# The next expert's weights split into a second pair of tiles, and copied in where the expert begins

## The chip, the cores and the metric

The kernel runs on one core of a Trainium2 chip. The metric is the device time of one launch in microseconds (us). TensorE is called PE (its weight loads PEld), VectorE DVE, ScalarE ACT, GpSimd POOL; SP issues most DMAs.

## The reference

An attention with a decaying state runs over 4 sequences of 768 tokens (8 heads of 48), and its output, 3072 rows of 384, is the input of a mixture of experts: each token goes to the one expert of 8 with the highest logit.

```
for t in range(S):
    cur = einsum('bhd,bhe->bhde', u * k_t, v_t)
    y[:, :, t] = einsum('bhd,bhde->bhe', r_t, state + cur)
    state = w * state + einsum('bhd,bhe->bhde', k_t, v_t)
...
e_idx = argmax(x @ w_gate + modality_bias[modality_id], axis=1)
for e in range(E):
    mask = e_idx == e
    h = maximum(x[mask] @ w1[e], 0)
    out[mask] = gate_w[mask] * (h @ w2[e])
```

With the inputs of the reference only three experts get tokens (1569, 1354 and 149).

## The kernel before

The first 220 us compute the attention, the choice of the expert and a sort: rows are written to DRAM by expert. Weights and activations are used as pairs of fp16 tiles (a high part and the rest), so that products of fp32 inputs are made with fp16 matmuls. An expert's weights are 128 x 6144 fp32 in `raw` (the first 3072 columns are the first layer's, the others the second's). `split` makes `whi` on ACT (raw times a power of two, rounded) and `wlo` on DVE (the rest), in six pieces of 1024 columns (NQ = 6); `norm` (L917) is the sum of squares of a piece on ACT, from which `scales` gets the power of two.

A job is 128 tokens of one expert. Ten jobs of the expert guessed to be the largest are worked in during the attention (L1036 to L1072). The remaining ones are numbered 0 to 15 here: job 0 stands ahead of a loop, jobs 1 to 15 are its iterations, with a bound read at run time (L1451). At run time the experts are sorted by size, and each has at least two jobs. Here the first has jobs 0 to 2, the second 3 to 13, the third 14 and 15; jobs 3 and 14 are the switches.

`jobs` (L792 to L896) is a chain of small DVE operations that makes a table with a column for each job: the row in DRAM, a code, and the expert to load. In the code, 8 says that the next job begins an expert, 4 that this one does; 2 and 1 ask for the norms of the second and the first half of the next weights. One fp32 matmul (`ptab`, L891) spreads the table; it stands in PE's order between the high and the low terms of the last of the ten early jobs. `jobs` is a generator; L1371 to L1397 say which of its steps stand between which of the other work.

One iteration, in the order in which each engine gets it (the order is written by hand, L1451, and each engine follows its own):

- `turn` (L989): SP fetches and transposes the rows of the job after;
- `low_terms` (L1082) of the job before: 8 matmuls with `hl` and the second layer's `whi`, the last of its `po`;
- `second_half`: if an expert begins, the second layer's weights are split, on ACT, DVE and POOL; else norms, if asked for;
- `put` (L959): ACT takes `po` to `otb` (L966), POOL scatters it to the output;
- `next_load`: if an expert begins, SP loads the next one's weights;
- `due` (L1087): the factors of the rows, on DVE;
- `up` (L1017): three groups of first-layer matmuls (L1006, 4, 2 and 2 blocks), each followed by `hh` on ACT (L1010) and `hl` on DVE (L1015); `scales` (a small matmul `pw`, L931, and four DVE operations) in between;
- `take_in` (L1408): two DVE copies of the next job's rows;
- `high_terms` (L1074): 16 matmuls with `hh`, `whi` and `wlo` of the second layer;
- `first_half`: if the next job begins an expert, the first layer's weights are split (ACT and DVE).

The code is read into a register of ACT, DVE and POOL at L900 (`at`). An If is a comparison and a branch on each of these engines. Where an If is not taken, its engine executes a stand-in (ALU_OP and EVENT_SEMAPHORE rows at the line of the If's end) that does the semaphore updates of what was skipped, since others wait for counts. At the loop's end all engines meet (L1505) before the last `low_terms`.

## Time and profile before

| | us |
|---|---|
| three runs: lowest, median, highest | 364.02, 365.57, 366.82 |
| the profiled execution, its span | 368.68, 367.0 |
| PE busy in the span | 337.0 (92%), clock 0.976 |
| DVE, ACT, POOL busy | 228.1, 157.0, 173.1 |
| job 0, first matmul | 224.58 |
| loop, first to last job's `ids` (L1091, 16 times) | 224.2 to 355.0 |
| last `low_terms` | 360.19 |
| norms in the loop (L917) | 323.79 to 335.55 |

An instruction's row of the profile has its start in us from the span's start, its duration in us, its engine, its line, the operation and its tiles; x24 says that 24 were merged, and what stands in brackets is the idle time of the engine before it and what ended it. Rows with a q behind the engine are of its sequencer (branches, register operations, semaphores): count, shortest/median/longest duration in ns, first and last start.

### The profile page before, as it was taken

To read this page: it belongs to the slowest core of one execution; us is meant where nothing else is said; L and a number is where in the kernel's file an instruction comes from. 1 tells how busy PE (TensorE), PEld (TensorE's weight loads), DVE (VectorE), ACT (ScalarE), POOL (GpSimd) and SP (SyncE) were. 2 spreads that over 40 slices of the span, in tenths; PEclk is the share of its full clock that TensorE was granted. 3 is DMA by queue.
4 is the path that set the end of the run, shared out by engine and by line. 5 is a ranking of instruction groups with operands and counts; after the bars stand their busy time and mean duration, and the time that the engine had idled before them with its cause. 6 is when DMAs were issued, how large, how long until landed. Compare 5 with 4: busy or idle time off the path is not lost. (4 is left out here: it accounts for less than half of the span.)

```text
span 367.0 us, 14637 instructions
## 1 busy us (share of the span) xinstructions
PE 337.0 (92%) x5314; PEld 266.4 (73%) x5314; DVE 228.1 (62%) x754; ACT 157.0 (43%) x371; POOL 173.1 (47%) x252
## 2 busy tenths in 40 slices
PE   7969999799999989989989699997999999999883
PEld 3758888589797787958767577775777888777661
DVE  6997777588969767697657443349533333324960
ACT  7237657435257664636632022236222222256711
POOL 7985656847876697565333411125111121111811
PEclk9998999969999999999999789999999999999999
DMA  6948999769799997965851413114912212112120
GB/s 157 246 123 241 278 258 235 198 146 203 222 228 167 234 307 153 206 182 138 241 129 46 129 45 46 43 43 134 273 49 54 53 43 64 43 22 64 22 55 4
DMA packets 56091, 50.66 MB, mean 138 GB/s; under 512 B 40936, under 2 KB 49641, under 8 KB 55792
## 3 DMA queue, kind: packets, MB, share of 16 engines
q1 hardware_dynamic: 52848, 40.60, 49.3%
q0 software_dynamic: 3200, 9.47, 7.0%
q8 instruction: 30, 0.49, 0.6%
q14 instruction: 13, 0.11, 0.1%
HBM read 30.55 MB, written 11.63 MB: 115 GB/s over the span
## 5 line engine op out<-in xcount | busy, mean ns | idle before, releaser
L1006 PEld LDWEIGHTS <-whi 128*128 128x128 f16 x1248 | 73.3, 98 | 8.4 <-issue 5.5
L1080 PEld LDWEIGHTS <-hh 128*128 128x128 f16 x416 | 38.6, 99 | 31.7 <-ACT hh L1010 5.9
L1006 PE MATMUL phb<-mxT,whi 128*128 128x128 f16 x720 | 47.6, 219 | 0.0
L1006 PEld LDWEIGHTS <-wlo 128*128 128x128 f16 x624 | 38.3, 99 | 4.4 <-DVE wlo L952 3.1
L1010 ACT ACTIVATE hh<-phb 128x256 f16<-128x256 f32 (+1 forms) x45 | 20.2, 453 | 42.2 <-PE po L1080 17.9
L1015 DVE SCALAR_TENSOR_TENSOR hl<-phb,hh 128x256 f16<-128x256 f32 (+1 forms) x45 | 22.8, 512 | 21.4 <-ACT hh L1010 11.5
L1006 PE MATMUL phs<-mxT,whi 128*128 128x128 f16 x480 | 31.7, 221 | 4.8 <-issue 4.8
L419 PE MATMUL psc<-rc,kc 48*64 48x128 f32 x768 | 30.5, 284 | 5.6 <-DVE settled L744 3.5
L345 POOL TENSOR_TENSOR rc<-ud,powr 128x512 f32<-128x512 f32 (+1 forms) x27 | 32.7, 1217 | 2.5 <-DMA ud<-in_pd 2.1
L648 POOL DMA_INDIRECT rows<-row,posi x24 | 24.2, 1010 | 19.1 <-issue 11.3
L530 ACT ACTIVATE row<-py,sx 128x384 f16<-128x384 f32 x24 | 13.9, 580 | 45.0 <-DVE sx L302 29.2
L425 DVE TENSOR_TENSOR at<-psc,mask 128x512 f32<-128x512 f32 x48 | 31.6, 681 | 0.2
L1085 PEld LDWEIGHTS <-hl 128*128 128x128 f16 x208 | 19.7, 97 | 15.5 <-issue 3.3
L1006 PE MATMUL phb<-mxT,wlo 128*128 128x128 f16 x360 | 28.0, 219 | 2.6 <-DVE wlo L952 2.6
L419 PEld LDWEIGHTS psc<-rc,kc 48*64 48x64 f32 x768 | 22.7, 136 | 10.3 <-issue 6.8
L454 PE MATMUL py<-kv,at 128*64 128x48 f32 x768 | 29.3, 229 | 0.9 <-issue 0.9
L454 PEld LDWEIGHTS py<-kv,at 128*64 128x64 f32 x768 | 27.4, 145 | 2.0 <-issue 1.7
L1090 DVE TENSOR_SCALAR fac<-mt,wf 128x1 f32<-128x1 f32 x16 | 3.4, 212 | 40.2 <-ACT otb L966 32.2
L1080 PE MATMUL po<-wlo,hh 128*128 128x384 f16 x128 | 26.3, 326 | 2.0 <-DVE wlo L952 2.0
L362 POOL TENSOR_TENSOR rk<-rc,kc 128x512 f32<-128x512 f32 x14 | 17.9, 1275 | 21.7 <-DVE ebx L300 9.8
L1080 PE MATMUL po<-whi,hh 128*128 128x384 f16 x128 | 27.1, 327 | 0.6 <-ACT hh L1010 0.6
L975 POOL TENSOR_TENSOR seenb<-otb,putb 128x1 int32<-128x1 int32 x15 | 2.8, 187 | 51.7 <-ACT otb L966 50.3
(268 smaller groups left out, 678.6 us busy)
## 6 DMA issues: line engine op xcount, KB each, us to landing
ud<-in_pd SPq DMA_DIRECT2D x48, 192.0 KB
kv<-in_pt SPq DMA_DIRECT2D x24, 384.0 KB
raw<-in_w SPq DMA_DIRECT2D x12, 512.0 KB
raw<-in_w SPq DMA_DIRECT2D x2, 1536.0 KB, 6.4
r<-in_pt SPq DMA_DIRECT2D x10, 192.0 KB
rows<-pad SPq DMA_DIRECT2D x1, 1544.0 KB
rows<-row,posi POOLq DMA_INDIRECT x24, 5.0
xn<-rows SPq DMA_TRANSPOSE x16
```

What stands on the lines that cost most here:

```text
L345: nc.gpsimd.tensor_mul(u["rc"][:, s], u["rT"][:, s], self.powr[:, s])
L362: nc.gpsimd.tensor_mul(u["rk"], u["rc"], u["kc"])
L419: nc.tensor.matmul(u["ps"][j][s, pr * P : (pr + 1) * P], u["kc"][r, pr, s], u["rc"][r, pr, :], start=True, stop=True)
L425: return nc.vector.tensor_mul(u["at"][:, j * NPR : (j + 1) * NPR, :], u["ps"][j].rearrange("p (q t) -> p q t", q=NPR), self.mask.unsqueeze ...
L454: nc.tensor.matmul(py[t, sl], u["at"][:, j * NPR + pr, t], u["v"][:, sl], start=c == h == 0, stop=h == H - 1 and i >= BARE, skip_group_che ...
L530: self.nc.scalar.activation(u["x16"][:, :DM], u["x"], AF.Copy, scale=u["g"]["sx"][:, b : b + 1])
L648: i = nc.gpsimd.indirect_dma_start(out=self.rows, out_offset=bass.IndirectOffsetOnAxis(ap=u["posi"][:, b : b + 1], axis=0), in_=u["row"][: ...
L1006: self.nc.tensor.matmul(ph[:, q * P : (q + 1) * P], w[:, c0 : c0 + P], self.xT[:, xq, t * P : (t + 1) * P], start=i == q == 0, stop=i == l ...
L1010: self.nc.scalar.activation(self.hh[:, f0 : f0 + fb, t * P : (t + 1) * P], p3, AF.Relu)
L1015: self.nc.vector.scalar_tensor_tensor(self.hl[:, f0 : f0 + fb, r], p3, 0.0, self.hh[:, f0 : f0 + fb, r], ALU.max, ALU.subtract)
L1080: self.nc.tensor.matmul(po[:, :DM], self.hh[:, f, t * P : (t + 1) * P], w[:, c0 : c0 + DM], start=n == q == f == 0, stop=False)
L1085: self.nc.tensor.matmul(po[:, :DM], self.hl[:, f, t * P : (t + 1) * P], self.whi[:, c0 : c0 + DM], start=False, stop=f == FB - 1)
```

## The change

The next expert's weights are split ahead of their expert's begin into a second pair of tiles, `nhi` and `nlo`, and copied from there to `whi` and `wlo` at the places where they were split before: the first layer's half at the end of the job ahead, the second layer's half behind the `low_terms` of the job that begins the expert. A copy of a half is four operations of 1536 columns: `whi` in two and the first half of `wlo` on DVE, the second half of `wlo` on ACT. POOL has no part in the split any more and reads no code.

The code has seven bits: 1, an expert begins in this job; 2, in the next one (copy of the first half); 4 and 8, norms of the first and the second half; 16 and 32, staging of the first and the second half; 64, staging of the first half in the same job as its copy (two jobs per expert in a row). As a rule norms stand five and four jobs ahead of an expert's begin, staging three and two. The table's arithmetic gets seven offsets in place of four and more operations. In each job `next_of` stands at the end, with three Ifs one behind the other (copy, staging, norms), and `first_of` stands where `second_half` was. For job 0, `next_of` stands inside the part whose order is written by hand.

```
--- before.py
+++ after.py
+OFFS = 7
...
-SP, ACT, AD = (mybir.EngineType.SP,), (mybir.EngineType.Activation,), (mybir.EngineType.Activation, mybir.EngineType.DVE, mybir.EngineType.Pool)
+SP, ACT, AD = (mybir.EngineType.SP,), (mybir.EngineType.Activation,), (mybir.EngineType.Activation, mybir.EngineType.DVE)
...
-        eq = new("eq", [P, 4, E])
-        v.scalar_tensor_tensor(eq, csm.unsqueeze(1).to_broadcast([P, 4, E]), self.line, self.grid, ALU.subtract, ALU.is_equal)
+        eq = new("eq", [P, OFFS, E])
+        v.scalar_tensor_tensor(eq, csm.unsqueeze(1).to_broadcast([P, OFFS, E]), self.line, self.grid, ALU.subtract, ALU.is_equal)
         yield
         field = new("field", [P, 4])
         v.scalar_tensor_tensor(field[:, ROW : ROW + 1], jr[:, 0:1], self.linep, jr[:, 1:2], ALU.add, ALU.min)
         v.scalar_tensor_tensor(nx[:, : E - 1], eid[:, 1:], float(E), act[:, 1:E], ALU.add, ALU.mult)
-        f, g = new("jf", [P, 4]), new("jg", [P, 4])
+        f, g = new("jf", [P, OFFS]), new("jg", [P, OFFS])
         v.reduce_sum(f, eq[:, :, 1:], axis=AX.X)
         v.reduce_sum(g, eq[:, :, 2:], axis=AX.X)
         yield
         v.scalar_tensor_tensor(field[:, SEEN : SEEN + 1], jr[:, 0:1], self.linep, field[:, ROW : ROW + 1], ALU.add, ALU.subtract)
-        last, now, soon, then = (slice(q, q + 1) for q in range(4))
-        a, b = new("ja", [P, 1]), new("jbit", [P, 1])
-        v.tensor_scalar(a, f[:, now], -1.0, 1.0, ALU.mult, ALU.add)
-        v.scalar_tensor_tensor(b, f[:, last], 2.0, g[:, soon], ALU.add, ALU.mult)
-        yield
-        v.scalar_tensor_tensor(b, g[:, then], a, b, ALU.mult, ALU.add)
+        col = lambda x, q: x[:, q + 1 : q + 2]
+        go, a, b, bits = new("jgo", [P, 1]), new("ja", [P, 1]), new("jb2", [P, 1]), new("jbits", [P, 5])
+        n1, n2, s1, s2, early = (bits[:, q : q + 1] for q in range(5))
+        v.tensor_scalar(go, col(f, 0), -1.0, 1.0, ALU.mult, ALU.add)
+        v.scalar_tensor_tensor(a, self.line, 0.0, col(f, -1), ALU.is_equal, ALU.max)
+        yield
+        v.tensor_tensor(n2, col(g, 2), col(g, 3), ALU.max)
+        v.tensor_mul(s2, col(f, 2), go)
         mr = new("mr", [P, E - 1])
         v.tensor_mul(mr, eq[:, 1, 1:], nx[:, 1:])
         yield
-        v.scalar_tensor_tensor(b, f[:, now], 4.0, b, ALU.mult, ALU.add)
+        v.tensor_tensor(n1, n2, col(g, 4), ALU.max)
+        v.tensor_mul(b, col(f, 2), a)
+        v.tensor_mul(early, a, col(f, 1))
+        v.tensor_mul(s1, col(f, 3), go)
+        yield
+        v.tensor_mul(bits[:, 0:2], bits[:, 0:2], col(f, 0).to_broadcast([P, 2]))
+        v.tensor_max(s2, s2, early)
+        v.tensor_max(s1, s1, b)
         v.reduce_sum(field[:, MORE : MORE + 1], mr, axis=AX.X)
         yield
-        v.scalar_tensor_tensor(field[:, CODE : CODE + 1], f[:, soon], 8.0, b, ALU.mult, ALU.add)
-        yield
+        v.tensor_max(n1, n1, col(g, 5))
+        v.tensor_max(n2, n2, col(g, 4))
+        code = field[:, CODE : CODE + 1]
+        v.scalar_tensor_tensor(code, early, 2.0, s2, ALU.mult, ALU.add)
+        yield
+        for bit in (s1, n2, n1, col(f, 1), col(f, 0)):
+            v.scalar_tensor_tensor(code, code, 2.0, bit, ALU.mult, ALU.add)
+            yield
         wide = [NJ, 4, NJ]
         d = new("jd", [P, 4, NJ])
...
         w = WQ // parts
         return slice(q * WQ + part * w, q * WQ + part * w + n * w), self.ws[:, 2 * q // NQ : 2 * q // NQ + 1]
-    def wide(self, q, part=0, parts=1, n=1):
-        sl, sc = self.piece(q, part, parts, n)
-        self.nc.scalar.activation(self.whi[:, sl], self.raw[:, sl], AF.Copy, scale=sc)
-    def fine(self, q, part=0, parts=1):
-        sl, sc = self.piece(q, part, parts)
-        self.nc.vector.scalar_tensor_tensor(self.wlo[:, sl], self.raw[:, sl], sc, self.whi[:, sl], ALU.mult, ALU.subtract)
-    def split(self, q, parts=1):
+    def split(self, q, parts=1, hi=None, lo=None):
+        hi, lo = (self.whi, self.wlo) if hi is None else (hi, lo)
         for part in range(parts):
-            self.wide(q, part, parts)
-            self.fine(q, part, parts)
+            sl, sc = self.piece(q, part, parts)
+            self.nc.scalar.activation(hi[:, sl], self.raw[:, sl], AF.Copy, scale=sc)
+            self.nc.vector.scalar_tensor_tensor(lo[:, sl], self.raw[:, sl], sc, hi[:, sl], ALU.mult, ALU.subtract)
     def put(self, po, t, key):
...
         take_in()
         po = self.ps_y.tile([P, 512], F32, tag="y", name="po")
         self.high_terms(po)
-        ms.close()
-        self.ordered = False
         self.actx.close()
         self.late = self.ctx.enter_context(tc.tile_pool(name="late", bufs=1))
         norms = lambda *qs: [self.norm(junk, q) for q in qs]
-        whole = self.late.tile([P, 768], F32, name="scaled")
-        def first_half(code):
-            with tc.If(code > 7):
-                for q in range(NQ // 2):
-                    self.split(q, 2 if q == 0 else 1)
-        def second_half(code):
-            with tc.If(code % 8 > 3) as first:
+        nhi, nlo = (self.late.tile([P, 2 * WC], F16, name=n, bufs=1) for n in ("nhi", "nlo"))
+        half = [slice(q * WC // 2, (q + 1) * WC // 2) for q in range(4)]
+        def moved(q):
+            for to, of in ((self.whi, nhi), (self.wlo, nlo)):
+                nc.vector.tensor_copy(to[:, half[2 * q]], of[:, half[2 * q]])
+            nc.vector.tensor_copy(self.whi[:, half[2 * q + 1]], nhi[:, half[2 * q + 1]])
+            nc.scalar.copy(self.wlo[:, half[2 * q + 1]], nlo[:, half[2 * q + 1]])
+        def first_of(code):
+            with tc.If(code % 2 > 0):
                 self.undo()
-                self.split(NQ // 2)
-                sl, sc = self.piece(NQ - 1, 0, 1)
-                lo, hi = slice(sl.stop - 768, sl.stop), slice(sl.stop - 512, sl.stop)
-                nc.gpsimd.tensor_tensor(whole, self.raw[:, lo], sc.to_broadcast([P, 768]), ALU.mult)
-                nc.gpsimd.tensor_tensor(self.whi[:, hi], self.raw[:, hi], sc.to_broadcast([P, 512]), ALU.mult)
-                mid = slice(sl.start - WQ, hi.start)
-                nc.scalar.activation(self.whi[:, mid], self.raw[:, mid], AF.Copy, scale=sc)
-                self.fine(NQ - 2)
-                rest = slice(sl.start, lo.start)
-                nc.vector.scalar_tensor_tensor(self.wlo[:, rest], self.raw[:, rest], sc, self.whi[:, rest], ALU.mult, ALU.subtract)
-                nc.gpsimd.tensor_tensor(self.wlo[:, lo], whole, self.whi[:, lo], ALU.subtract)
-            with first.Else():
-                with tc.If(code % 4 > 0):
-                    with tc.If(code % 2 > 0):
-                        norms(*range(NQ // 2))
-                    with tc.If(code % 4 > 1):
-                        norms(*range(NQ // 2, NQ))
+                moved(1)
+        def staged(q):
+            for q in range(q * NQ // 2, (q + 1) * NQ // 2):
+                self.split(q, 1, nhi, nlo)
+        def next_of(code):
+            with tc.If(code % 4 > 1):
+                with tc.If(code > 63):
+                    staged(0)
+                moved(0)
+            for bit, f in ((16, staged), (4, lambda q: norms(*range(q * NQ // 2, (q + 1) * NQ // 2)))):
+                with tc.If(code % (4 * bit) > bit - 1):
+                    for q in range(2):
+                        with tc.If(code % ((2 + 2 * q) * bit) > (1 + q) * bit - 1):
+                            f(q)
         def next_load():
             more = self.at(MORE, i, 2 * E - 1, SP)
             with tc.If(more > 0):
                 self.load(more % E, 2, 0, 1)
-        first_half(self.at(CODE, 0, 15, AD))
+        next_of(self.at(CODE, 0, 127, AD))
+        ms.close()
+        self.ordered = False
         with tc.For_i(1, nj, 1, iteration_sync="reg_based") as i, tc.manual_schedule(engines={getattr(mybir.EngineType, e) for e in MS[:4]}):
             self.turn(0, self.at(ROW, i, E * CAP, SP, 1), mn, xn)
-            code = self.at(CODE, i, 15, AD)
+            code = self.at(CODE, i, 127, AD)
             self.low_terms(po)
-            second_half(code)
+            first_of(code)
             self.put(po, 0, "b")
             next_load()
             self.due(m2, i)
...
             self.up("b", lambda: next(beside, lambda: None)(), True)
             take_in()
             self.high_terms(po)
-            first_half(code)
+            next_of(code)
         self.low_terms(po)
         self.put(po, 0, "c")
```

In `setup3` the tiles of the grid have 7 in place of 4 offsets.

## Prediction

> **What bounds the kernel now.** I read the page first (PE busy 92%), then the order of time of PE through the loop, then ACT's, then the sequencers' rows by source line. I call the 16 jobs 0 to 15 and T the start of a job's first L1006 matmul.

> ```profile
> 299.87 1.50 PE L1006 MATMUL phb<-mxT,whi 128*128 128x128 f16 x24
> ...
> 303.92 1.25 PE L1080 MATMUL po<-whi,hh 128*128 128x384 f16 x6
> ...
> 307.93 1.50 PE L1006 MATMUL phb<-mxT,whi 128*128 128x128 f16 x24
> ...
> 324.09 1.50 PE L1006 MATMUL phb<-mxT,whi 128*128 128x128 f16 x24
> ...
> 329.17 1.15 PE L1080 MATMUL po<-whi,hh 128*128 128x384 f16 x6 [0.56 <-ACT hh L1010]
> ```
> ```profile
> 248.53 1.52 PE L1006 MATMUL phb<-mxT,whi 128*128 128x128 f16 x24
> ...
> 251.52 0.68 PE L1006 MATMUL phb<-mxT,wlo 128*128 128x128 f16 x9 [1.31 <-DVE wlo L952]
> ...
> 259.65 1.51 PE L1006 MATMUL phb<-mxT,whi 128*128 128x128 f16 x24
> ```
> ```profile
> 333.08 1.50 PE L1006 MATMUL phb<-mxT,whi 128*128 128x128 f16 x24
> ...
> 341.02 1.54 PE L1006 MATMUL phb<-mxT,whi 128*128 128x128 f16 x24
> ...
> 352.45 1.55 PE L1006 MATMUL phb<-mxT,whi 128*128 128x128 f16 x24
> ```

> A plain job takes 307.93 - 299.87 = 8.06 us and PE has no gap in it: PE bounds the loop. Three jobs are longer. Jobs 3 and 14, in which the second and the third expert begin, take 11.12 and 11.43: PE waits there for the split (wlo). Job 12 takes 8.99: PE waits for ACT's hh. That is 3.06 + 3.37 + 0.93 = **7.36 us** above plain jobs, and all that the change can remove.

> How job 12 loses its 0.93 decides what the change is worth, so the reader should follow it closely:

> ```profile
> 305.37 0.38 ACT L1010 ACTIVATE hh<-phb 128x256 f16<-128x256 f32 x1 [0.76 <-PE po L1080]
> 308.37 0.58 ACT L966 ACTIVATE otb<-po,fac 128x384 f32<-128x384 f32 x1 [2.62 <-PE phb L1006]
> 310.45 0.60 ACT L1010 ACTIVATE hh<-phb 128x512 f16<-128x512 f32 x1 [1.50 <-PE phb L1006]
> ```
> ```profile
> 323.79 1.06 ACT L917 ACTIVATE junk<-raw 128x1024 f16<-128x1024 f32 x1 [1.88 <-PE po L1085]
> ...
> 327.12 0.19 ACT L917 ACTIVATION_READ_ACCUMULATOR junk<-raw 128x1 f32 x1
> 328.05 0.58 ACT L966 ACTIVATE otb<-po,fac 128x384 f32<-128x384 f32 x1 [0.74 <-PE L1006]
> 328.52 1.14 ACT L1010 ACTIVATE hh<-phb 128x512 f16<-128x512 f32 x3
> ```
> ```profile
> L1442 ACTq EVENT_SEMAPHORE  x1: 17/17/17, 327.3 to 327.3; - x1
> ```

> In a plain job ACT's last hh starts at T + 5.50, otb at T + 0.44 of the next job, the first hh at T + 2.52; PE needs that hh at T + 4.05 (303.92 - 299.87). ACT has 3512 ns of norms in job 12 (323.79 to 327.31). The branch behind them (L1442) is not taken, and its substitute for the skipped semaphore updates stands at 327.3, at the end of the norms, not when the sequencer reached it. Only then come otb (328.05), hh (328.52, done about 0.6 later) and PE (329.17). So **work on ACT or DVE ahead of an If that is not taken delays everything behind that If**: the sequencer doesn't run ahead.

> The sequencers' rows in plain job 9 price this control flow:

> ```profile
> L1424 ACTq ALU_OP  x1: 48/48/48, 306.7 to 306.7; - x1
> L1424 ACTq COMPARE_BRANCH  x1: 101/101/101, 306.8 to 306.8; - x1
> L966 ACTq FUSED_REGOPS  x1: 66/66/66, 307.6 to 307.6; - x1
> L1451 ACTq FUSED_REGOPS  x1: 79/79/79, 305.9 to 305.9; - x1
> L1424 DVEq ALU_OP  x2: 45/50/55, 307.8 to 308.7; - x2
> L1090 DVEq FUSED_REGOPS  x1: 53/53/53, 308.9 to 308.9; - x1
> L1419 DVEq EVENT_SEMAPHORE  x1: 21/21/21, 306.6 to 306.6; - x1
> ```

> On ACT two Ifs, not taken, last from 306.7 to 307.6: 0.45 each; I take 0.53 for one with its own modulus and semaphore. Loop end and reading the code last from 305.9 to 306.7: 0.85. On DVE two Ifs last from 307.8 to 308.9: 0.55 each; loop end and code 306.7 to 307.8: 1.1.

> **The change, part by part.** The second and third experts begin in jobs 3 and 14, so the new bits fall so: half 0 staged at the end of jobs 0 and 11, half 1 of 1 and 12, copies at the end of 2 and 13 and at the start of 3 and 14, norms at the end of 9 and 10.

> *Split leaves the switches; copies come in.* A copy is 128x1536 in fp16, three on DVE and one on ACT per half.

> ```profile
> L1408 DVE COPY mxT<-xn x16: 348/350/1367, 229.6 to 358.7; 128x768 f16<-128x768 f16 x16
> ```
> ```profile
> L947 ACT ACTIVATE whi<-raw,ws 128x1024 f16<-128x1024 f32 x6 | 6.4, 1133 | 0.0
> ...
> L1433 ACT ACTIVATE whi<-raw,ws 128x1536 f16<-128x1536 f32 x2 | 3.1, 1560 | 0.0
> ```
> ```profile
> L952 DVE SCALAR_TENSOR_TENSOR wlo<-raw,ws,whi x12: 737/1272/2302, 248.1 to 348.1; 128x1024 f16<-128x1024 f32 x8, 128x512 f16<-128x512 f32 x4
> ```

> Twice 350 is the upper end for a DVE copy (0.70), 0.35 the lower; I take 0.55, for part of the 350 is fixed. ACT's is 1.56, as L1433. The first copy starts at T + 6.9, behind DVE's take_in; whi's first half is there by T + 7.5, and PE wants it at T + 8.06; the other two by T + 8.6, wanted 1.3 and 2.0 us after the switch. The second group starts after low_terms and the control flow, at about T + 3.0 of the switch, and ends at T + 4.6; high_terms want the first at T + 4.05 and the last some 0.65 later. Hidden, with margins of a few tenths: I charge 0.5 for jobs 2, 3, 13 and 14 together (0 to 2.5). So 7.36 goes and 0.5 comes back. Loading raw no longer waits for the split; that is hidden before and after.

> *Norms, job 9.* Now they stand behind two Ifs, not taken, and ahead of one. From the last hh's start: 1.1 for two Ifs, 0.55 for two taken ones, 3.52 norms, 0.1 semaphore, 0.25 jump, 0.85 loop end and code, 0.54 for the If of the copies, 0.4 for otb's waits, 0.47 to hh, 0.6 for hh: 8.4, from T + 5.50, so T + 13.9, which is T + 5.85 of job 10. PE wants it at 4.05; as a late hh removes the small gap in high_terms (1.25 against 1.15 in the rows), the loss is **1.7** (1.2 to 2.0). Job 10's norms run last in their branch, and ACT has gained on PE by then: nothing.

> *Staging, jobs 0 and 11 (half 0).* ACT: three activations of 1.13 (L947, overlapping by 0.1): 3.2. DVE: first one ACT piece later, then three of L952's 1.27: 3.7. A not-taken If for half 1 stands behind, so DVE's chain counts: from ACT's last hh, 1.1 + 1.15 + 3.7 = 5.95, then 0.4 semaphore and jump, 0.45 the norms' If, 1.1 loop end and code, 0.65 the copies' If, whose release for the second layer's weights PE needs before high_terms: 8.55, T + 6.1 of job 12. Loss **2.0** in job 12 (1.1, if ACT's chain alone counted, to 2.4).

> ```profile
> 228.82 0.38 ACT L1010 ACTIVATE hh<-pha 128x256 f16<-128x256 f32 x1 [0.56 <-PE pha L1006]
> ```

> In job 0 ACT's last hh stands 3.7 ahead of job 1 (which begins at 248.53 - 2 x 8.0 = 232.5), against 2.56 in a plain job; the loop's entry takes some 0.8 more than its turn. Loss in job 1: **1.7** (1.0 to 2.2).

> *Half 1, jobs 1 and 12.* Same work, 6.8 to otb; but the job before was stretched, ACT stands 1.2 to 1.4 earlier against PE, and hh arrives about when PE wants it: in the 0.5 above.

> *The Ifs in every job.* Four on ACT and DVE where there were three. In plain jobs otb moves from T + 0.44 to T + 0.8, hidden by hh's T + 2.52; PE's release for the first layer's weights comes with the first If, at T + 6.7, before T + 8.06. No cost, except at the loop's exit, where all engines meet:

> ```profile
> 358.95 0.16 DVE L1408 COPY mt<-mn 128x4 int16<-128x4 int16 x1
> ```
> ```profile
> L1505 DVEq DRAIN  x2: 10/14/17, 359.6 to 360.2; - x2
> ```
> ```profile
> 360.19 1.46 PE L1085 MATMUL po<-whi,hl 128*128 128x384 f16 x8 [0.84 <-PEq L1505]
> ```

> DVE is the last to come (359.6) and PE's last low_terms wait for it. Two more Ifs behind mt: 0.65 + 0.45 = **1.1** (0.8 to 1.3). POOL no longer takes part in the Ifs; it was on no path.

> [...]

> *The table of jobs.* 23 small DVE operations where there were 9 before the table's matmul.

> ```profile
> 219.32 0.21 DVE L866 SCALAR_TENSOR_TENSOR field<-jr,linep,field 128x1 f32<-128x1 f32 x1
> ...
> 220.33 0.32 DVE L888 TENSOR_TENSOR jd<-field,id 40x160 f32<-40x160 f32 x1
> ```
> ```profile
> 222.80 0.54 PE L891 MATMUL ptab<-jd,ones 40*128 40x160 f32 x2
> ```

> Eight steps took 1.01, 0.13 each. Fourteen more, five of them in a chain (up to 0.19 each), are 1.6 to 2.1, and relu_low with its due (0.85) now stands ahead of the chain: jd ends between 223.1 and 223.6 where it ended at 220.65. PE wants it at 222.80. Cost 0.2 to 1.0; I take **0.6**.

> **Sum.** -7.36 + 0.5 + 1.7 + 2.0 + 1.7 + 1.1 + 0.6 = +0.2. The profiled execution took 368.68 (span 367.0, 1.7 around it); it would take 368.9. The median shown is 365.57, 3.1 below the profiled one; the same step puts it at **365.8**. With all lower ends the new costs are 4.3 (362.5), with all upper ends 11.4 (369.6).

> **Rivals.** *Stages hidden after all*: ACT and DVE run ahead past the Ifs, as they do at the switch before, where a branch that was taken needs no stand-in. For it: 3.2 and 3.7 us of work would fit in the 5.6 us between the last hh's end (T + 5.9) and the latest start of the next (T + 11.5). Against: L1442 at 327.3. Then 5.4 falls away: 360.4; half of it, 363.

> *Slower: the exit of the If tree becomes a gate for PE in each job.* If PE's release for the next job's first matmul comes behind all three Ifs, DVE gives it at T + 6.7 + 1.1 = 7.8, and PE wants it at 8.06. From 0.65 for each of the two it decides; at 0.8 each plain job loses 0.3, thirteen of them 4: 370. For it: DVE is the slowest sequencer. Against: each If carries its own semaphore (L1419 at 306.6).

> *Slower: instruction fetch.* The bodies grow by three stagings and two groups of copies, and branches jump over them.

> ```profile
> q1 hardware_dynamic: 14018, 6.00, 21.4%
> q0 software_dynamic: 960, 2.72, 5.3%
> ...
> out<-otb,putb POOLq DMA_INDIRECT x15, 2.6
> ```

> The first two rows are all DMA queues that moved anything between 232 and 358 us: no instruction packet, so the loop runs from what is loaded. If it no longer did, one fetch per job, priced as the small transfer in the last row (2.6 us from issue to landing) less about 1 of slack, would cost 15 x 1.6 = 24: 390. [...]

> *The change doesn't do what it says*: bits in other jobs, with the waits at the switches kept: 373. The table's arithmetic, followed for starts in jobs 3 and 14, speaks against it.

> **Chances.** About 1% (3.7 us) is what a measurement here can tell from no change. Forecast and its neighbours within 1%: 0.52. Stages hidden wholly or mostly: 0.24, faster by over 1%. Slower by over 1%: 0.24 (gate 0.12, margins at the switches lost 0.07, fetch 0.03, bits 0.02). The range 361.0 to 370.0 takes in the bounds and the nearer rivals.

> **What would show it.** Jobs 3 and 14 at 8.0 to 8.6 in place of 11.1 and 11.4; jobs 1, 10 and 12 at 9.5 to 10.1, with PE's idle time before L1080 ended by ACT hh or by DVE's copies' line; job 2 and plain jobs at 8.1; ptab's matmul about 0.6 after PE is ready; the last low_terms 1.1 later after mt than now (1.24). Jobs 10 and 12 at 8.1 prove my reading of the Ifs wrong; plain jobs over 8.2, the gate; a new wait for wlo in jobs 3 or 14, the margins.

## The result and the profile after

The changed kernel is slower: 378.62 us (median of 6; before 366.84, also 6), ratio 1.032 (95%: 1.028 to 1.036). Measured again later it was 378.23 against 367.13, ratio 1.028 (1.022 to 1.035). The forecast was 365.8, its range 361 to 370. The first profiled execution of the changed kernel was a disturbed one (545 us at a granted clock of 0.56), so the profile shown here is of that later measurement: 380.14 us, span 378.2, against 368.68 and 367.0 for the profile before.

Both traces can be cut at the first up matmul of each job. Job 0 starts at 224.05 (before 224.58), so nothing is lost ahead of the loop; from there to the end of the last low_terms it takes 148.51 us against 137.07. The two executions differ by 11.46, so the loss lies in the loop. By job, in us from one start to the next, "last" up to the end of low_terms:

| job | 0 | 1 | 2 | 3 | 4 | 5-9 | 10 | 11 | 12 | 13 | 14 | last |
|---|---|---|---|---|---|---|---|---|---|---|---|---|
| before | 7.94 | 7.95 | 8.06 | 11.13 | 7.99 | 40.29 | 8.06 | 8.10 | 8.99 | 7.95 | 11.43 | 9.20 |
| after | 13.91 | 8.91 | 9.70 | 9.34 | 8.20 | 39.92 | 9.46 | 7.94 | 12.10 | 7.96 | 9.33 | 11.76 |
| difference | +5.97 | +0.96 | +1.64 | -1.79 | +0.21 | -0.37 | +1.40 | -0.16 | +3.11 | +0.01 | -2.10 | +2.56 |

The two switches, jobs 3 and 14, gain 3.9 of the 6.4 that their waits cost. The largest loss stands between job 0 and job 1, where the forecast had 1.7 for a late hh in job 1 and nothing for a stop. PE in order of time (start, us, engine, line, operation):

```profile
230.37 0.49 PE L1086 MATMUL po<-wlo,hh 128*128 128x384 f16 x2
235.44 2.72 PE L1091 MATMUL po<-whi,hl 128*128 128x384 f16 x8 [4.58 <-DVEq L1458]
237.95 2.47 PE L1012 MATMUL phb<-mxT,whi 128*128 128x128 f16 x24
...
245.56 1.46 PE L1091 MATMUL po<-whi,hl 128*128 128x384 f16 x8
246.86 1.50 PE L1012 MATMUL phb<-mxT,whi 128*128 128x128 f16 x24
```

L1458 is the loop's entry. The operands of these low_terms (hl, whi) were there; PE stood for 4.58 us because DVE was still staging half 0 and gave its semaphore at the entry only then. DVE in order of time, then what the trace has of line L1458 on DVE:

```profile
229.32 0.16 DVE L1414 COPY mt<-mn 128x4 int16<-128x4 int16 x1
230.99 3.67 DVE L963 SCALAR_TENSOR_TENSOR nlo<-raw,ws,nhi 128x1024 f16<-128x1024 f32 x3 [1.51 <-ACT nhi L962]
```
```profile
L1458 DVEq EVENT_SEMAPHORE  x2: 21/21/21, 235.3 to 235.4; - x2
...
  PE po L1091: 4.6, 1
```

Staging ends at 234.66, the semaphore follows at 235.3, PE starts at 235.44. The work behind the stop is slow: low_terms take 2.72 where 1.46 is normal, the first 24 matmuls 2.47 instead of 1.50. The table of stretches says why. Its column after POOL is the granted TensorE clock:

```profile
224.00:230.80 6.80, 6.80 (x91) 5.51 (x88) 2.26 (x9) 2.94 (x5) 1.18 (x2) 1.00 0.46 62
230.80:235.40 4.60, 0.06 (x1) 0.00 (x0) 3.67 (x3) 2.23 (x3) 0.00 (x0) 0.75 0.01 4
235.40:240.20 4.80, 4.76 (x32) 3.45 (x32) 0.28 (x2) 0.58 (x1) 0.67 (x3) 0.52 0.20 41
240.20:246.00 5.80, 5.80 (x72) 4.62 (x70) 2.27 (x9) 1.40 (x4) 0.87 (x2) 1.00 0.09 34
```

The clock falls while PE stands and is 0.52 over almost 5 us of work; cut finer, it is 0.50 from 233.14 to 239.96 and 1.00 on both sides. So the stop costs 4.6 us and then 2.2 more (2.72 - 1.46 + 2.47 - 1.50).

The same pair, a stop and then a low clock (0.50 from 338.95 to 342.36 and from 369.67 to 373.08), makes job 12 and the exit so long:

```profile
337.93 1.14 PE L1086 MATMUL po<-whi,hh 128*128 128x384 f16 x6 [2.31 <-DVEq L1431]
338.90 2.08 PE L1086 MATMUL po<-wlo,hh 128*128 128x384 f16 x6
340.77 0.85 PE L1086 MATMUL po<-whi,hh 128*128 128x384 f16 x2
341.41 0.85 PE L1086 MATMUL po<-wlo,hh 128*128 128x384 f16 x2
342.05 1.62 PE L1091 MATMUL po<-whi,hl 128*128 128x384 f16 x8
...
369.83 2.72 PE L1091 MATMUL po<-whi,hl 128*128 128x384 f16 x8 [2.20 <-PEq L1512]
```

In job 12 the low clock costs 0.94 + 0.36 + 0.36 + 0.16 = 1.8, at the exit 1.26. In jobs 2, 3 and 14 PE waits for ACT, without a low clock; PE and then ACT, in order of time:

```profile
252.54 1.15 PE L1086 MATMUL po<-whi,hh 128*128 128x384 f16 x6 [1.47 <-ACT hh L1016]
...
256.56 1.50 PE L1012 MATMUL phb<-mxT,whi 128*128 128x128 f16 x24
...
261.99 1.15 PE L1086 MATMUL po<-whi,hh 128*128 128x384 f16 x6 [1.22 <-ACT hh L1016]
```
```profile
255.44 1.47 ACT L1428 COPY wlo<-nlo 128x1536 f16<-128x1536 f16 x1 [2.41 <-DVEq L1441]
259.50 1.47 ACT L1428 COPY wlo<-nlo 128x1536 f16<-128x1536 f16 x1 [2.58 <-PE phb L1012]
260.88 0.57 ACT L972 ACTIVATE otb<-po,fac 128x384 f32<-128x384 f32 x1
261.35 1.13 ACT L1016 ACTIVATE hh<-phb 128x512 f16<-128x512 f32 x3
```

ACT is late in job 2 behind the staging of half 1, and in job 3 its second copy (259.50 to 260.97) stands right ahead of otb and of the hh that PE waits for.

### The profile page after: what moved, and what is told of

It reads as the page before. It is cut to its first block, busy times and chain, and to the rows that moved or that the text cites. A ratio compares the mean times of both kernels' runs of the same rounds, so it can differ in the third digit from the quotient of the medians.

```text
span 543.2 us, 14784 instructions
## 1 busy us (share of the span) xinstructions
PE 532.2 (98%) x5314; PEld 391.1 (72%) x5314; DVE 229.7 (42%) x778; ACT 167.7 (31%) x375; POOL 160.7 (30%) x245
## 5 line engine op out<-in xcount | busy, mean ns | idle before, releaser
L1012 PEld LDWEIGHTS <-whi 128*128 128x128 f16 x1248 | 116.1, 130 | 10.4 <-issue 6.0
L1086 PEld LDWEIGHTS <-hh 128*128 128x128 f16 x416 | 53.6, 132 | 56.5 <-issue 51.5
L1012 PE MATMUL phb<-mxT,whi 128*128 128x128 f16 x720 | 77.3, 290 | 0.0
L1012 PEld LDWEIGHTS <-wlo 128*128 128x128 f16 x624 | 59.7, 130 | 2.5
L1012 PE MATMUL phs<-mxT,whi 128*128 128x128 f16 x480 | 49.3, 288 | 0.0
L1012 PE MATMUL phb<-mxT,wlo 128*128 128x128 f16 x360 | 43.5, 292 | 0.0
L1086 PE MATMUL po<-wlo,hh 128*128 128x384 f16 x128 | 43.4, 487 | 0.0
L1086 PE MATMUL po<-whi,hh 128*128 128x384 f16 x128 | 43.3, 485 | 0.0
L1091 PE MATMUL po<-whi,hl 128*128 128x384 f16 x128 | 40.0, 485 | 3.3 <-DVEq L1458 2.6
L455 PEld LDWEIGHTS py<-kv,at 128*64 128x64 f32 x768 | 40.1, 205 | 1.4 <-issue 0.9
L420 PEld LDWEIGHTS psc<-rc,kc 48*64 48x64 f32 x768 | 25.9, 143 | 10.5 <-POOL rc L346 2.2
```

The source lines that it names most:

```text
L420: nc.tensor.matmul(u["ps"][j][s, pr * P : (pr + 1) * P], u["kc"][r, pr, s], u["rc"][r, pr, :], start=True, stop=True)
L455: nc.tensor.matmul(py[t, sl], u["at"][:, j * NPR + pr, t], u["v"][:, sl], start=c == h == 0, stop=h == H - 1 and i >= BARE, skip_group_che ...
L1012: self.nc.tensor.matmul(ph[:, q * P : (q + 1) * P], w[:, c0 : c0 + P], self.xT[:, xq, t * P : (t + 1) * P], start=i == q == 0, stop=i == l ...
L1086: self.nc.tensor.matmul(po[:, :DM], self.hh[:, f, t * P : (t + 1) * P], w[:, c0 : c0 + DM], start=n == q == f == 0, stop=False)
L1091: self.nc.tensor.matmul(po[:, :DM], self.hl[:, f, t * P : (t + 1) * P], self.whi[:, c0 : c0 + DM], start=False, stop=f == FB - 1)
```

## The experiments

The pace differs between measurements: beside some runs the kernel before takes 366 to 367 us (after_third, best_act, best_head), beside the others 354 to 355. Each time is compared with that of the kernel before beside it. The changed kernel itself was not timed beside entry_warm, head, copy_dve, order, early0 and best, so what an edit does to it is read from the lengths of jobs, set against after_again, which has the same pace. They come from one profiled execution each, and tell more than the times, because what stands ahead of the loop varies by some us from run to run (job 0 starts at 215.32 in after_again and at 211.22 in copy_dve, whose edit lies behind that). Job lengths of the runs below (before: two further traces, from runs beside which before takes 355):

| kernel | job 0 | 1 | 2 | 3 | 4 | 10 | 12 | 13 | 14 | last | loop |
|---|---|---|---|---|---|---|---|---|---|---|---|
| before_again | 7.94 | 7.94 | 7.94 | 10.67 | 7.95 | 7.94 | 8.34 | 7.94 | 12.29 | 9.05 | 135.70 |
| table_pad | 7.95 | 7.94 | 7.94 | 10.54 | 7.95 | 7.94 | 8.34 | 7.94 | 10.90 | 9.55 | 134.67 |
| after_again | 13.91 | 9.11 | 9.38 | 9.33 | 8.17 | 8.81 | 10.41 | 8.60 | 9.33 | 9.82 | 144.55 |
| entry_warm | 13.09 | 9.19 | 9.36 | 9.34 | 8.14 | 8.80 | 10.42 | 8.60 | 9.33 | 13.92 | 147.86 |
| head | 7.95 | 9.78 | 9.68 | 8.27 | 8.24 | 9.00 | 9.56 | 9.61 | 8.26 | 9.04 | 137.25 |
| copy_dve | 13.91 | 9.22 | 9.13 | 8.93 | 7.95 | 8.58 | 12.07 | 7.94 | 8.19 | 9.82 | 143.42 |
| order | 12.76 | 8.33 | 8.69 | 8.92 | 8.67 | 7.94 | 8.41 | 8.87 | 8.85 | 9.78 | 138.92 |
| early0 | 8.22 | 7.95 | 9.14 | 8.61 | 8.46 | 8.96 | 9.93 | 8.50 | 8.63 | 9.73 | 135.79 |
| best | 7.92 | 7.94 | 7.95 | 7.94 | 7.94 | 7.94 | 7.94 | 8.13 | 7.94 | 9.71 | 129.05 |
| after_third | 13.91 | 8.91 | 9.70 | 9.34 | 8.20 | 9.46 | 12.10 | 7.96 | 9.33 | 11.76 | 148.51 |
| best_act | 7.92 | 7.96 | 8.48 | 8.60 | 8.89 | 8.56 | 8.39 | 8.25 | 8.60 | 10.80 | 134.32 |
| best_head | 9.14 | 7.94 | 9.12 | 8.05 | 7.94 | 8.38 | 9.46 | 9.16 | 8.06 | 9.17 | 134.65 |

**after_again**: the changed kernel once more, for a trace. 

> The changed kernel as it is, for a profile at an ordinary clock. If the chains of the Ifs are the cause (my theory), plain jobs stay at 8.1 us, jobs 1, 10 and 12 take 9.5 to 10.1, jobs 3 and 14 under 8.6, and some 11 us more are lost at places that I did not count: more jobs with late hh. If the end of the If tree gates PE (rival), plain jobs are 0.7 us or more above 8.06. If the loss lies ahead of the loop (rival), the first job begins 10 us later than at 224.58.

It took 367.3 us where before took 353.8. Its loop, 144.55, is 4.0 shorter than in the later trace; 3.1 of that are the low clock in job 12 and at the exit, which it escaped. The expectation was met for plain jobs (7.94) alone: jobs 1 and 10 (9.11, 8.81) stay under the 9.5 expected, 3 and 14 (9.33) and 12 (10.41) lie above, and no account in it had the stop of 4.59 at the entry.

**entry_warm.** Ahead of the loop:
```
         next_of(self.at(CODE, 0, 127, AD))
+        idle = self.ps_a.tile([P, 512], F32, tag="big", name="pidle")
+        for _ in range(20):
+            nc.tensor.matmul(idle, self.ones16, self.warm, start=True, stop=True)
         ms.close()
```

> The changed kernel with 20 idle 512-column matmuls on PE between job 0's high_terms and the loop's entry, where PE stood still for 4.59 us; nothing reads their result. Theory (the stop itself lowers the granted clock): the wait for DVE at the entry stays, but the low_terms and the first 24 up matmuls behind it take 1.46 and 1.50 us again in place of 2.72 and 2.67, so the kernel takes 2 to 2.5 us less than the changed one: 10.5 to 11.5 us above before, where the changed kernel was 13.5 above. Rival (the matmuls behind the entry are slow because code or weights arrive late there): both stay at 2.7, and the time stays 13 to 14 above.

Measured: 367.01 against 355.28, ratio 1.036 (1.027 to 1.044). It did not test what it was meant to: 19 of the 20 matmuls came to stand behind the loop (they take 4.26 us there, which is the long last job), and PE stood at the entry as before. That the stop itself lowers the clock rests on the clock's own record, here too (stretch 225 to 227, granted clock 0.50), not on an intervention; between the theory and its rival this run decides nothing.

**head.**
```
+            ahead(code)
             self.low_terms(po)
             first_of(code)
...
             next_of(code)
```
Here ahead has the Ifs of staging and norms for the job before, and next_of keeps those of the copies alone; the bits stand one job later in the table.

> The changed kernel with the Ifs for staging and norms moved from the end of a job to the head of the next one, inside the loop (the bits stand one job later in the table); the If of the copies stays at the end. Theory (at the loop's entry all engines meet, so PE waited for staging that it did not need): the 4.59 us wait and the low clock behind it go, job 0 takes 8 to 8.5 instead of 13.9; the loop's end no longer stands behind the staging, so job 12 takes 9 to 9.6 instead of 10.4 and the exit gets 0.5 to 1 shorter. In all 7 to 10 less than the changed kernel: 4 to 6 above before. Rival 1 (the entry waits for something else, such as code to be loaded): the wait stays at 3 us or more and the time at 11 to 13 above. Rival 2 (the staging is simply too long for a job): what job 0 gains comes back in job 1, which takes 12 to 13.

Measured: 359.66 against 355.28, ratio 1.017 (1.007 to 1.026). Job 0 takes 7.95: the wait at the entry is gone, so it was for the staging, not for the entry. The exit is 0.78 shorter. Rival 2 holds in part: jobs 1, 2, 12 and 13 take 9.6 to 9.8, with staging now ahead of the copies' If (L1433), for whose stand-in PE waits in jobs 1, 2 and 13. PE in order of time:

```profile
228.15 1.14 PE L1088 MATMUL po<-whi,hh 128*128 128x384 f16 x6 [1.21 <-DVEq L1433]
...
350.11 1.46 PE L1093 MATMUL po<-whi,hl 128*128 128x384 f16 x8 [0.77 <-PEq L1517]
```

**copy_dve.**
```
-            nc.scalar.copy(self.wlo[:, half[2 * q + 1]], nlo[:, half[2 * q + 1]])
+            nc.vector.tensor_copy(self.wlo[:, half[2 * q + 1]], nlo[:, half[2 * q + 1]])
```

> The changed kernel with the one copy that ACT made in each group (second half of wlo) on DVE. Theory (in jobs 3 and 14 the 1.47 us copy on ACT stands ahead of otb and hh, and PE waits 1.2 for that hh): jobs 3 and 14 take 8.0 to 8.4 instead of 9.33, the time falls by 1.5 to 2.5 to 11 to 12 above before. Rival (ACT's hh is late there because of the control flow, and DVE's fourth copy of 0.55 makes hl as late): both jobs stay at 9.0 to 9.4, no change within 0.5.

Measured: 364.74 against 355.28, ratio 1.032 (1.022 to 1.040), 9.5 above before where 11 to 12 was expected. The loop is 1.1 shorter than in after_again. Job 14 falls from 9.33 to 8.19, as the theory had it; job 3 only to 8.93: PE waits 0.54 there for DVE's first copy of the second group. Job 12, which the edit does not touch, hides the gain: after a stop of the usual length the clock fell. PE in copy_dve, then in after_again, the same place:

```profile
323.10 1.86 PE L1086 MATMUL po<-whi,hh 128*128 128x384 f16 x6 [2.29 <-DVEq L1431]
324.75 2.13 PE L1086 MATMUL po<-wlo,hh 128*128 128x384 f16 x6
```
```profile
328.22 1.14 PE L1086 MATMUL po<-whi,hh 128*128 128x384 f16 x6 [2.31 <-DVEq L1431]
329.19 1.14 PE L1086 MATMUL po<-wlo,hh 128*128 128x384 f16 x6
```

**order.** Each choice becomes an If with its Else, norms first (cut):
```
+            with tc.If(code % 16 > 3) as some:
...
+            with some.Else():
+                with tc.If(code % 64 > 15):
...
+                        with tc.If(code % 64 > 31) as late:
+                            staged(1)
+                        with late.Else():
+                            staged(0)
```

> The changed kernel with the Ifs of norms and staging written so that none that is not taken stands behind a staging or a norm: each choice is an If with its Else, norms first, and a job does norms or staging, not both (this routing never asks for both in one job). Theory (each If not taken behind the work costs 0.45 to 0.65 because its stand-in waits until the engine has drained): jobs 12, 13 and 10 shorten by 0.5 to 1.2 each, 1.5 to 2.5 in all, 11 to 12 above before. Rival (the length of staging and norms decides, the Ifs run alongside): no change within 0.5.

Measured: 359.68 against 355.28, ratio 1.011 (1.006 to 1.016); the profiled execution took 361.77. More than the theory said: job 12 falls by 2.0, job 10 by 0.9, jobs 1 and 2 by 0.7 to 0.8, jobs 3 and 14 by 0.4 to 0.5, the stop at the entry from 4.59 to 3.44; jobs 4 and 13 get 0.3 to 0.5 longer. In all the loop is 5.6 shorter than in after_again. The work is the same, so what was removed is control flow behind it. How it adds up is seen in after_third's job 12, where the staging on DVE starts at 331.27 and lasts 3.68, to 334.95; then, from DVE's sequencer rows by line:

```profile
L1447 DVEq EVENT_SEMAPHORE  x1: 21/21/21, 335.0 to 335.0; - x1
```
```profile
L1445 DVEq COMPARE_BRANCH  x2: 75/100/126, 335.5 to 335.9; - x2
L1445 DVEq ALU_OP  x1: 55/55/55, 335.4 to 335.4; - x1
```
```profile
L913 DVEq TENSOR_LOAD <-tab x1: 316/316/316, 336.9 to 336.9; - x1
```
```profile
L1431 DVEq COMPARE_BRANCH  x1: 119/119/119, 337.4 to 337.4; - x1
L1431 DVEq EVENT_SEMAPHORE  x1: 21/21/21, 337.9 to 337.9; - x1
...
  PE po L1086: 2.3, 1
```

The If for the other half is not taken and its stand-in waits for the end of the staging (335.0); the norms' If (335.4), the loop's end, the load of the code (336.9) and the If of the copies follow one by one, and only the last stand-in (337.9) lets PE go on: 2.9 us in which DVE computes nothing.

**before_again**: the kernel before, for a trace from the chip of the next three. 

> The kernel before, once more, for a trace from the chip of the next three. The loop (first up matmul of job 0 to the last low_terms) takes 137.07 us as in the first trace, within 0.3. What stands before the loop is a static program; where its time differs from the first trace and from run to run, the chip or the granted clock decides, not the change. If the static part of the changed kernels is really slower by the 2 to 4 us that their medians leave over beside the loop, its first up matmul of job 0 stands 2 to 4 earlier here than theirs on this chip.

Loop 135.70, 1.4 under the first trace, where 0.3 was allowed; its plain jobs take 7.94 without the small gaps, and job 14 12.29 where table_pad, with the same loop, has 10.90. Job 0 starts at 211.65.

**early0.**
```
         self.s_up(9, 0)
+        self.scales("1")
...
         self.s_due(9)
+        for q in range(NQ // 2):
+            sl, sc = self.piece(q, 0, 1)
+            nc.scalar.activation(nhi[:, sl], self.raw[:, sl], AF.Copy, scale=sc)
...
+        for q in range(NQ // 2):
+            sl, sc = self.piece(q, 0, 1)
+            nc.vector.scalar_tensor_tensor(nlo[:, sl], self.raw[:, sl], sc, nhi[:, sl], ALU.mult, ALU.subtract)
         self.up("a")
```

> The changed kernel, in which half 0 of the second expert is staged before the loop without an If, in the idle time of ACT and DVE beside the last two static jobs (ACT's three pieces behind the last hh of slot 9, DVE's three behind the first due; the scales are worked out one slot earlier); at the loop's entry only Ifs that are not taken remain. Theory (PE waits at the entry for whatever DVE still has to do, and the stop lowers its clock): job 0 takes 8.3 to 9 instead of 13.9 and job 1 8.3 to 9.1, the loop 139 to 140 instead of 144.6: 5 to 6 less than the changed kernel. Rival (the entry itself, or code that is loaded there, stops PE): job 0 stays over 11.

Measured: 358.02 against 355.25, ratio 1.009 (1.004 to 1.014). Job 0 takes 8.22, job 1 7.95, the loop 135.79, 8.8 less than the changed kernel in after_again, where 5 to 6 was expected. With no stop the clock stays, too (1.00 from 220 to 228). PE in order of time:

```profile
222.30 1.46 PE L1091 MATMUL po<-whi,hl 128*128 128x384 f16 x8
223.59 1.50 PE L1012 MATMUL phb<-mxT,whi 128*128 128x128 f16 x24
```

**best** (early0, order and copy_dve together). 

> The same early staging of half 0 together with the ordering of the Ifs (none not taken behind a staging or a norm) and all copies on DVE. If the three causes are independent: the loop of the ordered kernel, 138.9, less 4 for job 0 and less 1 to 1.5 for jobs 3, 4 and 14: 133 to 134.5, 2.5 to 4 under the loop of before (137.07). Then the kernel is 1 to 4 us faster than before, if what stands ahead of the loop costs no more than 2. Rival (the causes overlap: what one edit removes was hidden behind another): loop 135 to 137 and no difference that can be measured.

Measured: 353.14 against 355.25, ratio 0.992 (0.988 to 0.996): faster than the kernel before. The loop takes 129.05, below what the three edits promised singly: every job but one is at 7.92 to 7.95, and from job 0 on PE's order of time shows a single wait, at the exit:

```profile
342.14 1.46 PE L1091 MATMUL po<-whi,hl 128*128 128x384 f16 x8 [1.44 <-PEq L1537]
```

The loop is 6.65 us shorter than in before_again, the kernel only 2. Its job 0 starts at 214.56, 2.9 later than in before_again. Of that, matmul against matmul, 1.55 stood at 200 us already, ahead of anything that was edited, where traces of one kernel differ as much. Nearly all of the rest is a wait for the table of jobs, in the stretch into which the early staging was put:

```profile
212.81 0.51 PE L904 MATMUL ptab<-jd,ones 40*128 40x160 f32 x2 [1.28 <-DVE jd L901]
```

early0, best_act and best_head have this wait too (1.28, 1.39 and 1.72), the kernels without early staging at most the 0.23 of table_pad: it comes with the early staging. A further 2.3 lies outside the profile's span: in all 12 runs of best the time is 3.9 to 4.5 longer than the span, in the runs of before beside it 1.7 to 2.2. What takes it is not shown.

**table_pad.**
```
+        for n in range(9):
+            v.tensor_mul(more[:, n % 7 : n % 7 + 1], f[:, now], g[:, soon])
...
+        for n in range(5):
+            v.scalar_tensor_tensor(more[:, 7:8], more[:, 6:7] if n == 0 else more[:, 7:8], 2.0, b, ALU.mult, ALU.add)
```

> The kernel before with 14 more small DVE operations in the table of jobs ahead of jd, nine apart and five in a chain, whose result nothing reads: only the longer table of the change. Prediction's step: 0.6 us (0.2 to 1.0). Theory now (jd ends just as PE wants it): 0 to 0.5. Rival (the 2 to 4 us that the changed kernels lose ahead of their loops is the table): 2 to 4 us slower than before.

Measured: 353.95 against 355.25, ratio 0.998 (0.994 to 1.002). The theory holds: PE waits 0.23 for the longer table, no more:

```profile
211.58 0.54 PE L899 MATMUL ptab<-jd,ones 40*128 40x160 f32 x2 [0.23 <-DVE jd L896]
```

**after_third**: the profile shown above. 

> The changed kernel unchanged, on the chip of the next two. The loop takes 144 to 145 us as in its first usable trace, 9 to 10 more than before's on these chips (135.70 and 134.67). Theory (the loss lies in the loop, and what stands ahead of it varies by itself): the kernel is 9 to 12 us slower, and its first up matmul of job 0 can stand anywhere between 211 and 216. Rival (a further 3 to 4 us are lost ahead of the loop by the change): 12 to 14 slower, first up matmul at 215 or later.

Ratio 1.028; 11 slower, as the theory had it. The loop, 148.51, is longer than the 144 to 145 expected; 3.1 of it are the low clock in job 12 and at the exit. Job 0 starts at 224.05, but both bounds for it were set for the other pace. The profile before, of the same pace, has 224.58, so the rival falls: ahead of the loop the change costs nothing that can be seen.

**best_act** (best with the copy on ACT). 

> The kernel with early staging and ordered Ifs, but with the fourth copy of a group on ACT again, as the change had it. Theory (ACT's copy makes hh late at the switches, whatever stands around it): jobs 3 and 14, and the one behind each, lose 0.5 to 1.2, the loop takes 130.5 to 132 instead of 129.05, the time 1.5 to 2.5 more than with all copies on DVE. Rival (ACT was late only because of the Ifs behind the work): 129 to 129.5 and no difference.

Measured: 365.24 against 367.13, ratio 0.994 (0.991 to 0.998). PE waits for ACT's hh in jobs 3, 4 and 14, where best has no wait:

```profile
252.03 1.15 PE L1086 MATMUL po<-whi,hh 128*128 128x384 f16 x6 [0.49 <-ACT hh L1016]
260.93 1.15 PE L1086 MATMUL po<-whi,hh 128*128 128x384 f16 x6 [0.77 <-ACT hh L1016]
...
342.59 1.15 PE L1086 MATMUL po<-whi,hh 128*128 128x384 f16 x6 [0.48 <-ACT hh L1016]
```

That speaks for the theory, but jobs 2, 10 and 12 are 0.4 to 0.6 longer as well and the exit 1.1 (0.6 of wait and 0.5 of low clock), which the copy does not explain; where before takes 367, its own trace has longer jobs also (job 12 8.99 against 8.34). In time the two cannot be told apart across measurements.

**best_head** (best with the Ifs of staging and norms at the head). 

> Early staging, ordered Ifs and all copies on DVE, with the Ifs of staging and norms at the head of the next job, so that the last job leaves none behind. Theory (each If on DVE behind the last mt delays the loop's exit): the last job to the end of low_terms takes 9.0 to 9.2 instead of 9.71 and the rest stays, loop 128.4. Rival (staging right ahead of otb and hh makes hh late, as in the first kernel with the Ifs at the head): jobs 1, 12 and 13 take 8.5 to 9.6, loop 130 to 133, slower than with the Ifs at the end.

Measured: 366.23 against 367.13, ratio 0.998 (0.995 to 1.002). The last job takes 9.17, but jobs 0, 2, 12 and 13 9.1 to 9.5. In jobs 2, 12 and 13 PE waits (0.9 to 1.2 in each) behind the work at the head, so there the rival is right. Job 0 has no wait: its first 24 matmuls take 2.72, at a granted clock of 0.50 that fell behind the wait of 1.72 for the table. By the lengths of jobs the end is the better place; in time best_head is 1.0 slower than best_act, measured beside the same before, and the intervals overlap.

## Why the prediction was wrong

The loop was forecast 0.4 shorter (without the table) and is 11.4 longer. Of these 11.8, 5.2 come from jobs 0 and 1, 3.9 from half 1 and the copies, 2.0 from job 12, 1.5 from the exit; norms and plain jobs take 0.8 less than forecast.

**Job 0's staging.** The step that failed first is "the loop's entry takes some 0.8 more than its turn", with a loss of 1.7 in job 1. The entry was priced as a few more instructions on ACT and DVE. It is a place where PE waits for DVE, whatever PE's own operands say: 4.58 of stop and 2.2 of low clock, 6.9 in jobs 0 and 1 (5.97 + 0.96). The prediction had the fact in hand, for the exit: "where all engines meet". head and early0 take the staging away from the entry, by two different ways, and job 0 falls to 7.95 and 8.22. The late hh that was forecast for job 1 did not come: its 0.96 is the low clock.

**Half 1 and the copies.** "Hidden, with margins of a few tenths: I charge 0.5." The runs show 1.64 in job 2, 1.3 each in jobs 3 and 14 over a plain 8.06, and 0.21 in job 4: 4.4. The copies were timed rightly (DVE 0.55 to 0.56, ACT 1.47 against 1.56) and whi and wlo are there in time. What was not followed is the ACT copy's own place: it stands ahead of otb and hh of the same job, and copy_dve takes 1.1 from job 14 by moving it. For job 2 the reason given was that the job before would be stretched and ACT so be ahead of PE; but the loss stood at the entry, before job 1's first matmul, ACT had gained nothing in job 1, and PE waited 1.47 for its hh. For job 13 the reason held (+0.01, behind a job 12 that was stretched by 3.1); in after_again job 13 takes 8.60.

**Staging in job 12.** Right in mechanism and place: DVE's chain ends last and PE waits for the stand-in behind the copies' If. The forecast was 2.0 of loss; the stop is 2.31. The low clock adds 1.8 in this trace (none in after_again, where the job takes 10.41).

**Norms in job 10**: 1.7 forecast, 1.40 measured over before (1.34 of wait for hh). **Exit**: 1.1 forecast; the wait grew from 0.84 to 2.20 here (1.55 in after_again; 0.77 in head, where no such Ifs stand behind the last job), plus 1.26 of low clock. **Plain jobs**: no cost forecast; 39.92 for five against 40.29. These terms held, but for the clock at the exit. **Table**: 0.6 forecast; in the changed kernel ptab's matmul (222.27 in after_third) has no wait before it, in table_pad 0.23. This term was too large.

**The term that was missing** is the clock. 2.2 + 1.8 + 1.26 = 5.3 of the 11.4 us are matmuls that ran at a granted clock of 0.50 behind a stop. Every stop was counted at its own length.

**The rivals.** Stages hidden after all: fell. order shows what kept them from it, and best that they can be hidden when nothing that is not taken stands behind them and half 0 is staged ahead of the loop. The gate in each job: fell, plain jobs take 7.97. Instruction fetch: fell, with plain jobs as short as before and job 0 at 8.22 once its staging is out of the way. From the stop at the entry on, the changed kernel has two instruction packets, at 234.6 and 235.2, when the stop at the entry had lasted 3.8 us, and none from 235.4 to 372.5; the row of its DMA queues for 232 to 363 us:

```profile
q14 instruction: 2, 0.02, 0.0%
```

The bits stand in the jobs that the table's arithmetic gave.

The record of a branch is not the price of an If. In the rows of DVE shown for order a branch takes 75 to 126 ns, but three Ifs, a loop's end and a load take 2.9 us there, from the end of the staging (335.0) to the last stand-in (337.9).

**Left open**: no run moves a stop against the grid or fills one with matmuls, so the link between idle time and clock is read from the traces and not shown by an intervention.

## What to carry to other kernels

Work that can be hidden inside this loop, as best shows, was not hidden at its entry and exit: in after_third PE stood there for 4.58 and 2.20 us, at the entry for DVE, which came last with its 3.67 of staging. So price what is put in front of an entry as time in which PE stands. It belongs earlier, as in best, and what it pushes back there has to be priced too. A stop of PE cost more than its length where the clock fell behind it, up to 2.2 us more; in this loop that took 2.0 us of standing in one window of 3.41. Put nothing that is not taken behind work in a branch (order's loop is 5.6 us shorter than after_again's for this): write choices as If and Else with the work last, and price the whole way from the end of the work to the next release, not the single branch.

## What the hardware showed beside that

The same stop cost 1.4 us more in one trace and not in another. In job 14 of before, PE waits 2.0 for wlo; in before_again the clock fell, in table_pad, with the same loop, it did not. PE in order of time, before_again and then table_pad; then the windows of the grid in each (us, PE busy, PEld, DVE, ACT, POOL, granted clock):

```profile
334.02 0.81 PE L1080 MATMUL po<-wlo,hh 128*128 128x384 f16 x4 [2.01 <-DVE wlo L952]
334.67 0.79 PE L1080 MATMUL po<-whi,hh 128*128 128x384 f16 x2
...
335.88 2.58 PE L1085 MATMUL po<-whi,hl 128*128 128x384 f16 x8
```
```profile
335.60 0.81 PE L1088 MATMUL po<-wlo,hh 128*128 128x384 f16 x4 [2.02 <-DVE wlo L960]
336.24 0.49 PE L1088 MATMUL po<-whi,hh 128*128 128x384 f16 x2
...
336.89 1.75 PE L1093 MATMUL po<-whi,hl 128*128 128x384 f16 x8
```
```profile
331.31:334.72 3.41, 1.40 (x10) 0.73 (x8) 3.41 (x6) 0.09 (x1) 3.26 (x3) 1.00 0.00 0
334.72:338.13 3.41, 3.41 (x13) 1.57 (x12) 2.03 (x9) 0.00 (x0) 0.71 (x2) 0.50 0.09 33
```
```profile
331.00:334.41 3.41, 2.58 (x30) 1.90 (x30) 3.41 (x3) 1.26 (x4) 3.28 (x2) 1.00 0.00 0
334.41:337.83 3.42, 2.12 (x13) 1.06 (x13) 3.28 (x11) 0.00 (x0) 2.26 (x3) 1.00 0.07 28
```

In before_again the whole stop lies in one window (2.01 of standing), in table_pad it is parted (0.83 and, with small gaps behind it, 1.30). Job 14 takes 12.29 and 10.90. The fall also came after the stop, at the end of the window: in job 12 of after_third the stop ends at 337.93 and the window at 338.95, so the first six matmuls behind it ran at full speed (1.14) and the next six took 2.08. So a difference of 1 to 2 us between two traces of these kernels can be this alone, and has to be looked for in the durations of the matmuls before it is put down to an edit.
